# Batch 0's attention: normalising the output by spread row sums, alternating heads, and an earlier end of its rest

## The chip, the cores and the metric

The kernel runs on one core of a Trainium2 chip, as one launch. The metric is the device time of that launch in microseconds (us). The engines are PE (TensorE, the matrix engine, with PEld its weight loads), DVE (VectorE), ACT (ScalarE), POOL (GpSimd) and SP (which here issues DMA transfers). Each runs its own queue of instructions strictly in the order in which the program issued them, and waits at semaphores for the others.

## The reference, cut to what matters

```python
def _attn_ref(q, k, v, n_global, n_local):      # batch 2, heads 8, seq 768, head_dim 64
    scores = scale * np.matmul(q, k.transpose(0, 1, 3, 2))
    keep = is_global | is_local                  # 8 global keys, a band of 96 keys
    scores = np.where(keep, scores + bias, -1000000000.0)
    scores = scores - np.max(scores, axis=-1, keepdims=True)
    a = np.exp(scores)
    a = a / (np.sum(a, axis=-1, keepdims=True) + 1e-09)
    return np.matmul(a, v)

def _moe_ref(x, w_gate, w1, w2):                 # x 1536 x 512, 8 experts, d_ff 1024
    P = np.exp(x @ w_gate - max)                 # then 8 rounds of row and column sums
    for e in range(8):
        out += P[:, e:e + 1] * (np.maximum(x @ w1[e], 0.0) @ w2[e])

def _moe2_ref(x, w_in, w_out):                   # d_ff 2048
    h = x @ w_in
    return (h * (1.0 / (1.0 + np.exp(-1.702 * h)))) @ w_out
```

The attention's output, both batches under one another, is the x of the experts, and their sum is the x of the last network.

## The kernel before, in words

All products are of fp32 operands split into a high and a low part; each product is three matmuls (high by low, low by high, high by high). The first layer of every expert is done with seven products of block sums instead of eight products of blocks (operands of the tokens are B11, B21, B22, T1 to T4, those of the weights A11, A12, S1 to S4; each has an h and an l part).

**The attention** (`attention_banded`) goes through 48 works in order. A work is a batch b, a head pair hp (two heads, on partitions 0 to 63 and 64 to 127) and a tile i of 128 queries; a head pair has six works. For a step n of the loop the order of issue in the first phase is `ORDER[1] = "tsvrn"`:

- t, `turn` of work n - 3: the probabilities `a` are transposed on PE into a PSUM tile `pt` (L913) and, from i = 2 on, their columns for the global keys into `pg` (L921); ACT copies them to `ah` (L916) and `ag` (L925).
- s, `scores` of work n: for each head j three matmuls (L876) into a tile `s`, then DVE adds the bias and takes the row's extreme (L889), then ACT takes the exponential and sums the rows into `rs` (L892).
- v, `values` of work n - 4: PE multiplies by the values into `pv` (L954); after an odd i `put_x` copies two tiles' worth of it with ACT into the token matrix `xf` (L726, two copies of 64 partitions by 256).
- r, the rest of `turn`: DVE makes the low part `al` from `pt` and `ah` (L934).
- n, `norm` of work n - 1: DVE adds 1e-9 to the row sums (L899), takes the reciprocal (L900) and scales `a` with it, once for each head (L902).

Behind a work with i = 1 or i = 4, `prep_qk` transposes the next three tiles of keys and queries: PE into `pk` and `pq` (L812, L818), ACT into `kh` and `qh` (L813, L823), DVE into `kl` and `ql` (L814, L824), POOL copies the global keys (L827).

PSUM has eight banks, in four pools: `ps_s` 2, `ps_t` 2, `ps_v` 1, `ps_m` 3. `psum(kind)` says which pool a tile takes. In the first phase the scores go to m, and "p" (`pk`, `pq`) to s. `pt` and `pg` are both of kind "t". A tile can be written only when the readers of the tile that had its bank before are done.

**The phases.** In phase 1 PE does the attention of batch 0 and the first works of batch 1, up to the values of (0, 3, 3); meanwhile DVE, ACT and POOL already prepare the first weights (`first_weights`) and the first operands of the tokens of batch 0 (B11, T1). Then comes `mixture`: layer 1 of the first unit of an expert, with a list of side work that is issued between its products: the rest of batch 0's attention, then its last operands (`operands0`: B21, B22, T2, T3, T4), then batch 1's attention, and so on. `need(name)` issues all side work up to that name on the spot. In the scores of phase 1 one head's three matmuls stand before the other's; in phase 2 the heads alternate.

The first products of layer 1 are, in order, x (A11 by B11, tile `pl1x`), z (S1 by T1, `pl1z`), x again (A12 by B21) and y (S2 by T2, `pl1y`), all at L462.

Of the kernel before, what the change touches and what calls it, by code (L numbers as in the profile page):

```python
# [7 lines left out]
F32 = mybir.dt.float32  # L8
# [3 lines left out]
AF = mybir.ActivationFunctionType  # L12
ALU = mybir.AluOpType
# [3 lines left out]
P = 128  # L17
GK = 32
# [5 lines left out]
LT, LV = 3, 4  # L24
# [24 lines left out]
class Kernel:  # L49
# [495 lines left out]
    def psum(self, kind, shape, name):  # L545

        if kind == "2":
            self.turnover += 1
            kinds = {2: "m", 3: "sst", 4: "sstt"}[self.phase]
            kind = kinds[self.turnover % len(kinds)]  # L550
        elif self.phase == 1:
            kind = {"s": "m", "p": "s"}.get(kind, kind)
        kind = "t" if kind == "p" else kind
        p = {"s": self.ps_s, "t": self.ps_t, "v": self.ps_v, "m": self.ps_m}[kind]
        return p.tile(shape, F32, tag=kind, name=name)

# [69 lines left out]
    def mixture(self, side):  # L626


        side = list(side)
        done = set()  # L630
        debt = [0.0]

        def advance(steps=None):
            if not side:
                return
            debt[0] += side[0][2] if steps is None else steps
            while debt[0] >= 1 and side:
                debt[0] -= 1
                name, g, _ = side[0]
                try:  # L640
                    next(g)
                except StopIteration:
                    done.add(name)
                    side.pop(0)

        def need(name):
            while any(n == name for n, _, _ in side):
                advance(1.0)

        self.need = need  # L650
        self.ahead_done = False
        steps = self.steps
        NV = len(self.versions)
        nx = self.nx
        prev = None

        def second(step):
            v, u, b, lastv = step
            turn = (v, u) == self.ends[b]
            if turn and b == 0:  # L660
                self.xf2 = [self.xfp.tile([P, self.DC, self.S], F32, tag="xf", name="xf2_0")]
            for t, _ in enumerate(self.layer2(v, u, b)):
                advance()
                if turn and t >= LR:
                    self.retranspose(b, t - LR)
            if turn:
                side.insert(0, (f"again{b}", again(b), (1.2, 1)[b]))
            if lastv and v + 1 < NV:
                self.split_w2(v + 1)
                self.load_w2(v + 3)  # L670

        def again(b):

            self.operands_open(b, (self.xp0, self.xp1)[b], self.acc[b])
            for t in range(self.NT - LR, self.NT):
                self.retranspose(b, t)
                yield
            yield from self.operands(b, self.xf2[b], fine=True)

        for i, (v, u, b) in enumerate(steps):  # L680
            lastv = i + 1 == len(steps) or steps[i + 1][0] != v
            if u == 0 and b == 1:
                need("operands1")
            if (v, u) == self.ends[b] and b == 1:
                need("doubles")
                self.last()
            if (v, u) == self.starts[b]:
                need(f"again{b}")
            n = 0
            for k in self.layer1(v, u, b, first=i == 0):  # L690
                if i == 0 and n == 2:
                    need("operands0")
                if lastv and v + 1 < NV and n >= 1:
                    self.split_w1(v + 1, last)
                last = k
                n += 1
                advance()
            if lastv and v + 1 < NV:
                self.split_w1(v + 1, last)
                self.load_w1(v + 3)  # L700
                for _ in self.sum_weights(v + 2):
                    pass
            if prev is not None:
                combined = prev[1] == self.ue and prev[2] == 1
                if combined:
                    need("sinkhorn")
                second(prev)
                if prev[1] == 2 * self.ue - 1 and prev[2] == 0:
                    self.ahead_done = True
                if combined:  # L710
                    self.late()
                    side.append(("doubles", self.doubles(self.cv), 0.42))
            prev = (v, u, b, lastv)
        second(prev)


    def put_x(self, pv, b, hp, i):


        nc = self.nc  # L720
        if hp == 0 and i == 1:
            self.xf = self.xfp.tile([P, self.DC, self.S], F32, tag="xf", name=f"xf_{b}")
        ts_ = slice((i - 1) * P, (i + 1) * P)
        for j in range(2):
            r = slice(64 * j, 64 * j + 64)
            nc.scalar.activation(self.xf[r, hp, ts_].rearrange("p (s t) -> p s t", s=2), pv[r, :, j, :], AF.Copy)  # L726

    def slope(self, h):
        return 2.0 ** -(8.0 * (h + 1) / self.H)
# [1 line left out]
    def attention_open(self, ctx):  # L731
        nc, tc = self.nc, self.tc
# [3 lines left out]
        self.a_q = pool("a_q", 2)  # L736
        self.a_v = pool("a_v", 3)
        self.a_m = pool("a_m", 4)
        c = self.a_c

        self.bias = c.tile([P, 2 * W], F32, name="bias")
# [110 lines left out]
    def scores(self, b, hp, i):  # L852

        nc = self.nc
# [7 lines left out]
        else:  # L862
            keys, bias, wn = lambda x: x[:, (i - 1) * SLOT : (i - 1) * SLOT + W], self.bias[:, P : P + W], W
        a = self.a_a.tile([P, 2, W], F32, tag="a", name=f"a_{b}_{hp}_{i}")
        rs = self.a_m.tile([P, 2], F32, tag="rs", name=f"rs_{b}_{hp}_{i}")

        rows = [slice(64 * j, 64 * j + 64) for j in range(2)]
        passes = [(ql, self.kh), (qh, self.kl), (qh, self.kh)]
# [6 lines left out]
            x, y = passes[n]  # L875
            nc.tensor.matmul(o, x[rows[j], i % 3, :], keys(y[rows[j]]), start=(n == 0), stop=(n == 2))  # L876

        if self.phase > 1:
            for n in range(3):
                for j in range(2):  # L880
                    product(j, n)
        for j in range(2):
            if self.phase == 1:
                for n in range(3):
                    product(j, n)
            s = a[:, j, :wn]
            o, x = (pairs(s, P), pairs(ps[j], P)) if i == 1 else (s, ps[j])
            m = self.a_m.tile([P, 1], F32, tag="m", name=f"m_{b}_{hp}_{i}_{j}")
# [2 lines left out]
            )  # L891
            nc.scalar.activation(s, s, AF.Exp, bias=m, scale=-1.0, accum_out=rs[:, j : j + 1])  # L892
            yield
        self.aa[b, hp, i] = a, rs, wn

    def norm(self, b, hp, i):
        nc = self.nc
        a, rs, wn = self.aa[b, hp, i]
        nc.vector.tensor_scalar(rs, rs, 1e-9, None, op0=ALU.add)  # L899
        nc.vector.reciprocal(rs, rs)  # L900
        for j in range(2):
            nc.vector.tensor_scalar(a[:, j, :wn], a[:, j, :wn], rs[:, j : j + 1], None, op0=ALU.mult)  # L902

    def turn(self, b, hp, i):

# [10 lines left out]
        nc.scalar.activation(ah[:, :n], pt, AF.Copy)  # L916
        ag = None
        if i >= 2:
            pg = self.psum("t", [GK, 2, P], f"pg_{b}_{hp}_{i}")
            for j in range(2):  # L920
                nc.tensor.transpose(pg[:, j, :], a[:, j, P:SLOT], self.ident)  # L921

# [17 lines left out]
    def values(self, b, hp, i):  # L940
# [12 lines left out]
        for n, (x, y) in enumerate(mm):  # L953
            nc.tensor.matmul(o, x, y, start=(n == 0), stop=(n == len(mm) - 1))  # L954
        if i % 2 == 1:
            self.put_x(self.pv, b, hp, i)

    def attention_banded(self):

        nc = self.nc  # L960
        self.aq, self.av, self.vg = {}, {}, {}
        self.aa, self.at = {}, {}
        pairs = [(b, hp) for b in range(self.B) for hp in range(self.HP)]
        work = [(b, hp, i) for b, hp in pairs for i in range(self.NT)]
        tables = self.tables()
# [6 lines left out]
        for n in range(len(work) + LV):  # L972
# [3 lines left out]
            for o in ORDER[self.phase]:  # L976
# [5 lines left out]
                    rest = self.turn(*work[n - LT])  # L982
                if o == "n" and 1 <= n <= len(work):
                    self.norm(*work[n - 1])
                if o == "r" and rest is not None:
                    rest()
                    yield
# [257 lines left out]
```

## Time and profile before

| what | before |
|---|---|
| time, median of 3 runs (lowest to highest) | 1463.09 us (1460.62 to 1464.42) |
| run that was profiled | 1463.75 us, of which 1461.8 us is the span from the first to the last instruction |
| granted TensorE clock, mean over the span | 0.987 |
| busy, share of the span | PE 96%, DVE 69%, POOL 60%, ACT 44% |
| chain that ended last | PE 70% of the span |

The time lies 1.95 us above the span in the profiled execution. The first phase lasts until about 95 us, a fifteenth of the span; the rest is nearly all the experts' products. The granted clock is 1.00 at 2.4 GHz and about half at 1.2 GHz.

### The profile page before, as it was taken

How to read it: one execution, taken by the hardware profiler on the slowest of the kernel's cores; microseconds unless marked ns; L12 is line 12 of the kernel's file. 1: busy time of each engine (PE TensorE's matmuls, PEld its weight loads, DVE VectorE, ACT ScalarE, POOL GpSimd, SP SyncE). 2: the span in 40 equal slices, each digit the busy share in tenths (PEclk: the TensorE clock that was granted, in tenths of full speed). 3: DMA queues.
4: the chain of work that ended last, by engine and by line, in shares of the span. 5: the costliest groups of instructions: out<-in, count | busy, mean ns of one | idle time of the engine just before them, and what ended most of it. 6: DMA issues, size and time to landing. Idle time of an engine off the chain costs nothing.

```text
span 1461.8 us, 20827 instructions
## 1 busy us (share of the span) xinstructions
PE 1409.9 (96%) x7295; PEld 1244.0 (85%) x7295; DVE 1005.5 (69%) x1847; ACT 642.1 (44%) x1511; POOL 870.7 (60%) x1003
## 2 busy tenths in 40 slices
PE   7899999998999999999999999999999979999998
PEld 5667888787899998998998998998989868899897
DVE  7987887577567777677777777767754466556655
ACT  5676766343443333333333343343334456444332
POOL 4745555657685556655566555666556596666642
PEclk9989999999999999999999999999999999999999
DMA  6322210111122222212222212222101110111002
GB/s 158 79 49 62 74 47 30 58 59 58 58 88 86 73 87 73 81 57 73 72 87 66 86 63 68 77 83 87 44 29 44 44 44 29 44 41 32 30 0 87
DMA packets 94225, 91.62 MB, mean 63 GB/s; under 512 B 41888, under 2 KB 71584, under 8 KB 94112
## 3 DMA queue, kind: packets, MB, share of 16 engines
q1 hardware_dynamic: 94112, 90.21, 19.7%
q8 instruction: 59, 0.97, 0.3%
q14 instruction: 54, 0.44, 0.1%
HBM read 78.66 MB, written 11.53 MB: 62 GB/s over the span
## 4 chain that ended last, share of the span: by engine, by line
PE 70%; DVE 2%; ACT 1%; POOL 1%; issue 1%; DVEq 0%; ACTq 0%
PE pl L515 37%; PE pl1x L462 9%; PE pl1y L462 9%; PE pl1z L462 9%; PE pl1w L462 5%; DVE sg L431 1%; ACT sg L428 0%; DVE acc L526 0%; DVE acc L298 0%; PE pr L542 0%; ACT hh L210 0%; DVE p L416 0%; POOL s L203 0%; DVE u L416 0%; POOL hl L216 0%
## 5 line engine op out<-in xcount | busy, mean ns | idle before, releaser
L515 PE MATMUL pl<-w2h,hl 128*128 128x512 f32 x960 | 303.6, 398 | 14.2 <-DVE accx L524 5.4
L526 DVE SCALAR_TENSOR_TENSOR acc<-pl,pr,acc 128x512 f32<-128x512 f32 x312 | 233.2, 749 | 120.8 <-PE pl L515 118.9
L515 PE MATMUL pl<-w2l,hh 128*128 128x512 f32 x960 | 299.5, 393 | 1.0 <-POOL w2l L216 1.0
L515 PE MATMUL pl<-w2h,hh 128*128 128x512 f32 x960 | 298.8, 393 | 0.0
L216 POOL TENSOR_TENSOR w2l<-r,w2h 128x512 fp32r<-128x512 f32 x100 | 133.6, 1357 | 191.2 <-ACT w2h L210 177.0
L515 PEld LDWEIGHTS pl<-w2h,hl 128*128 128x128 f32 x960 | 177.0, 189 | 49.1 <-DVE accx L524 6.6
L515 PEld LDWEIGHTS pl<-w2l,hh 128*128 128x128 f32 x960 | 181.7, 189 | 41.4 <-POOL w2l L216 1.9
L515 PEld LDWEIGHTS pl<-w2h,hh 128*128 128x128 f32 x960 | 181.5, 189 | 39.0
L210 ACT ACTIVATE w2h<-r 128x512 fp32r<-128x512 f32 x98 | 56.5, 624 | 201.6 <-PE pl L515 163.2
L438 POOL TENSOR_TENSOR hl<-u,hh 128x384 fp32r<-128x384 f32 x100 | 108.6, 1094 | 36.9 <-ACT hh L435 36.6
L469 ACT ACTIVATE p<-pl1x 128x384 f32<-128x384 f32 x80 | 39.2, 490 | 160.4 <-PE pl1x L462 147.6
L438 POOL TENSOR_TENSOR hl<-p,hh 128x384 fp32r<-128x384 f32 x50 | 50.8, 1015 | 97.0 <-ACT hh L435 97.0
L416 DVE TENSOR_TENSOR u<-p,pl1y 128x384 f32<-128x384 f32 x86 | 47.5, 552 | 79.0 <-PE pl1y L462 67.6
L216 POOL TENSOR_TENSOR hl<-sg,hh 128x384 fp32r<-128x384 f32 x64 | 67.1, 1049 | 54.9 <-ACT hh L210 54.1
L434 ACT ACTIVATE p<-p 128x384 f32<-128x384 f32 x50 | 26.3, 526 | 134.9 <-DVE p L416 134.9
L216 POOL TENSOR_TENSOR S3l<-s,S3h 128x256 fp32r<-128x256 f32 x50 | 38.5, 770 | 75.6 <-ACT S3h L210 62.9
L443 DVE SCALAR_TENSOR_TENSOR hl<-pl1x,hh 128x384 fp32r<-128x384 f32 x64 | 35.6, 557 | 66.7 <-ACT hh L440 66.3
L203 POOL TENSOR_TENSOR s<-r 128x256 f32<-128x256 f32 x100 | 78.8, 788 | 0.0
L434 ACT ACTIVATE u<-u 128x384 f32<-128x384 f32 x100 | 51.9, 519 | 50.7 <-DVE u L416 50.5
L892 ACT ACTIVATE a<-a,m 128x288 f32<-128x288 f32 (+2 forms) x96 | 48.1, 501 | 42.5 <-DVE m L889 42.5
L532 DVE TENSOR_TENSOR acc<-pl,acc 128x512 f32<-128x512 f32 x84 | 54.2, 682 | 13.8 <-PE pl L515 12.7
L216 POOL TENSOR_TENSOR A22l<-r,A22h 128x256 fp32r<-128x256 f32 x50 | 45.0, 900 | 24.0 <-ACT A22h L210 24.0
(266 smaller groups left out, 3415.9 us busy)
## 6 DMA issues: line engine op xcount, KB each, us to landing
r<-in_moe_w_dram SPq DMA_DIRECT2D x82, 512.0 KB, 3.5
r<-d SPq DMA_DIRECT2D x18, 512.0 KB, 3.7
d<-in_moe_w_in_dram SPq DMA_DIRECT2D x16, 512.0 KB, 4.5
d<-cx SPq DMA_DIRECT2D x32, 256.0 KB, 2.2
d<-in_moe_w_out_dram SPq DMA_DIRECT2D x16, 512.0 KB, 4.3
out_dram<-acc SPq DMA_DIRECT2D x12, 256.0 KB, 2.0
k<-in_k_dram SPq DMA_DIRECT2D x28, 96.0 KB, 2.3
q<-in_q_dram SPq DMA_DIRECT2D x28, 96.0 KB, 2.4
```

The costliest lines, as they stand in the source:

```text
L203: nc.gpsimd.tensor_tensor(out=o, in0=x, in1=y, op=op)
L210: nc.scalar.activation(hi, x, AF.Copy)
L216: e.tensor_tensor(out=lo, in0=x, in1=f(hi), op=ALU.subtract)
L416: add = lambda o, x, y: nc.vector.tensor_tensor(out=o, in0=x, in1=y, op=ALU.add)
L434: nc.scalar.activation(c, c, AF.Relu)
L438: nc.gpsimd.tensor_tensor(out=l, in0=c, in1=f(h), op=ALU.subtract)
L462: nc.tensor.matmul(ps, x[:, d, :], y[:, d, :], start=(new and i == 0 and d == 0), stop=(i == 2 and d == 1), skip_group_check=True)
L469: nc.scalar.activation(p1, ps, AF.Copy)
L515: nc.tensor.matmul(ps, x[:, c, ts_], y, start=(i == 0 and c == 0), stop=(i == 2 and c == 1))
L526: nc.vector.scalar_tensor_tensor(out=acc, in0=ps, scalar=self.pr[:, tt, e : e + 1], in1=acc, op0=ALU.mult, op1=ALU.add)
L532: nc.vector.tensor_tensor(out=acc, in0=ps, in1=acc, op=ALU.add)
L892: nc.scalar.activation(s, s, AF.Exp, bias=m, scale=-1.0, accum_out=rs[:, j : j + 1])
```

## The change

It has four parts.

1. `psum`: in phase 1 "p" (`pk`, `pq`) takes banks of m, which the scores also take, and the new kind "g" (`pg`, and the new `pb`) takes those of s. `pt` has the two t banks for itself.
2. `scores`: the heads' products alternate in phase 1 too.
3. For batch 0 the probabilities are no longer scaled. The row sums of two works (i even and odd) lie in one tile `rs` of 128x4; behind the odd one `norm` adds 1e-9 and takes the reciprocal once, and POOL spreads the four columns to `rw`, 128x256 (each 64 times). `spread`, right behind the `turn` of the odd work, transposes `rw` on PE into `pb` (two transposes, L923) and ACT copies it to `rb` (L925 of the changed kernel). `put_x` then multiplies `pv` by `rb` on DVE (L730, two of 64x256) instead of copying it on ACT. Batch 1 stays as it was.
4. In the first layer 1 the rest of batch 0's attention and `operands0` are issued behind the first product instead of the third.

```diff
-            kind = {"s": "m", "p": "s"}.get(kind, kind)
-        kind = "t" if kind == "p" else kind
+            kind = {"s": "m", "p": "m", "g": "s"}.get(kind, kind)
+        kind = "t" if kind in "pg" else kind
...
-                if i == 0 and n == 2:
+                if i == 0 and n == 0:
                     need("operands0")
...
-            nc.scalar.activation(self.xf[r, hp, ts_].rearrange("p (s t) -> p s t", s=2), pv[r, :, j, :], AF.Copy)
+            o = self.xf[r, hp, ts_].rearrange("p (s t) -> p s t", s=2)
+            if rb is None:
+                nc.scalar.activation(o, pv[r, :, j, :], AF.Copy)
+            else:
+                nc.vector.tensor_tensor(out=o, in0=pv[r, :, j, :], in1=rb[r], op=ALU.mult)
...
-        if self.phase > 1:
-            for n in range(3):
-                for j in range(2):
-                    product(j, n)
+        for n in range(3):
+            for j in range(2):
+                product(j, n)
         for j in range(2):
-            if self.phase == 1:
-                for n in range(3):
-                    product(j, n)
...
-        nc.vector.tensor_scalar(rs, rs, 1e-9, None, op0=ALU.add)
-        nc.vector.reciprocal(rs, rs)
+        if b == 0 and i % 2 == 0:
+            return
+        o = rs.rearrange("p s j -> p (s j)") if b == 0 else rs[:, i % 2]
+        nc.vector.tensor_scalar(o, o, 1e-9, None, op0=ALU.add)
+        if b == 0:
+            w = self.a_b.tile([P, 4, self.D], F32, tag="rw", bufs=1, name=f"rw_{b}_{hp}_{i}")
+            nc.vector.reciprocal(o, o)
+            nc.gpsimd.tensor_scalar(w, o[:, :, None].to_broadcast([P, 4, self.D]), 1.0, 1.0, op0=ALU.mult, op1=ALU.mult)
+            self.rb[b, hp, i] = w
+            return
+        nc.vector.reciprocal(o, o)
         for j in range(2):
-            nc.vector.tensor_scalar(a[:, j, :wn], a[:, j, :wn], rs[:, j : j + 1], None, op0=ALU.mult)
+            nc.vector.tensor_scalar(a[:, j, :wn], a[:, j, :wn], o[:, j : j + 1], None, op0=ALU.mult)
+
+    def spread(self, b, hp, i):
+        nc = self.nc
+        w = self.rb[b, hp, i].rearrange("p s d -> p (s d)")
+        pb = self.psum("g", [P, 2, P], f"pb_{b}_{hp}_{i}")
+        for s in range(2):
+            nc.tensor.transpose(pb[:, s, :], w[:, s * P : s * P + P], self.ident)
+        rb = self.a_b.tile([P, 2, P], F32, tag="rb", name=f"rb_{b}_{hp}_{i}")
+        nc.scalar.activation(rb, pb, AF.Copy)
+        self.rb[b, hp, i] = rb
...
-            pg = self.psum("t", [GK, 2, P], f"pg_{b}_{hp}_{i}")
+            pg = self.psum("g", [GK, 2, P], f"pg_{b}_{hp}_{i}")
...
+                if o == "t" and LT <= n and n < len(work) and work[n - LT][0] == 0 and work[n - LT][2] % 2 == 1:
+                    self.spread(*work[n - LT])
```

Three places show how instructions move. In their rows the batch is left out of a name: `s_1_2_0_19899` is the score tile of head pair 1, tile 2, head 0, and the last number is that of the buffer.

PE in phase 1, head pair 1, behind the preparation of its second half of keys and queries, before the change:

```order
L812 MATMUL pk_19861<-ident,k_19604 128x128 x3
L818 MATMUL pq_19867<-ident,q_19607 128x128 x3
L913 MATMUL pt_0_5_19884<-ident,a_0_5_19732 128x128 x4
L921 MATMUL pg_0_5_19892<-ident,a_0_5_19732 32x128 x2
L876 MATMUL s_1_2_0_19899<-kh,ql_19708 128x288
L876 MATMUL s_1_2_0_19899<-kl,qh_19707 128x288
L876 MATMUL s_1_2_0_19899<-kh,qh_19707 128x288
L876 MATMUL s_1_2_1_19906<-kh,ql_19708 128x288
L876 MATMUL s_1_2_1_19906<-kl,qh_19707 128x288
L876 MATMUL s_1_2_1_19906<-kh,qh_19707 128x288
```

The same place in the changed kernel:

```order
L817 MATMUL pk_19854<-ident,k_19602 128x128 x3
L823 MATMUL pq_19860<-ident,q_19605 128x128 x3
L937 MATMUL pt_0_5_19877<-ident,a_0_5_19730 128x128 x4
L945 MATMUL pg_0_5_19885<-ident,a_0_5_19730 32x128 x2
L923 MATMUL pb_0_5_19890<-ident,rw_0_5_19808 128x128 x2
L883 MATMUL s_1_2_0_19897<-kh,ql_19706 128x288
L883 MATMUL s_1_2_1_19899<-kh,ql_19706 128x288
L883 MATMUL s_1_2_0_19897<-kl,qh_19705 128x288
L883 MATMUL s_1_2_1_19899<-kl,qh_19705 128x288
```

The two transposes of `pb` have come in ahead of the scores, and the second head's first product stands right behind the first head's. `pk`, `pq` and the two score tiles follow one another through the three banks of m, so the second score tile takes the bank that `pk` had.

DVE in phase 1, around the end of head pair 1, before:

```order
L889 ISA a_2_1_20144,m_2_1_1_20157<-s_2_1_1_20153,bias 128x256
L889 ISA m_2_1_1_20157 128x1
L934 TENSOR_TENSOR al_1_4_20137<-pt_1_4_20131,ah_1_4_20136 128x512
L899 TENSOR_SCALAR rs_2_0_20099<-rs_2_0_20099 128x2
L900 RECIPROCAL rs_2_0_20099<-rs_2_0_20099 128x2
L902 TENSOR_SCALAR a_2_0_20098<-a_2_0_20098,rs_2_0_20099 128x128 x2
L814 TENSOR_TENSOR kl<-pk_20178,kh 128x3x128
L824 SCALAR_TENSOR_TENSOR ql_20189<-pq_20184,qs,qh_20188 128x384
```

And in the changed kernel:

```order
L892 ISA a_2_1_20142,m_2_1_1_20154<-s_2_1_1_20145,bias 128x256
L892 ISA m_2_1_1_20154 128x1
L730 TENSOR_TENSOR xf_19751<-pv_1_2_20116,rb_1_3_20094 64x256 x2
L958 TENSOR_TENSOR al_1_4_20135<-pt_1_4_20129,ah_1_4_20134 128x512
L819 TENSOR_TENSOR kl<-pk_20171,kh 128x3x128
L829 SCALAR_TENSOR_TENSOR ql_20182<-pq_20177,qs,qh_20181 128x384
```

The scaling between `al` and `kl` is gone, and the two multiplications of `put_x` have come in ahead of `al`.

PE at the start of the mixture, before (the products x and z, then the scores and transposes of the attention, then x again):

```order
L462 MATMUL pl1x_0_20844<-B11h_20288,A11h_20000 128x384 x2
L812 MATMUL pk_20857<-ident,k_20543 128x128 x3
L818 MATMUL pq_20863<-ident,q_20546 128x128 x3
L462 MATMUL pl1z_0_20879<-T1h_20296,S1l_20201 128x384 x2
L462 MATMUL pl1z_0_20879<-T1l_20297,S1h_20200 128x384 x2
L462 MATMUL pl1z_0_20879<-T1h_20296,S1h_20200 128x384 x2
L876 MATMUL s_0_2_0_20892<-kh,ql_20684 128x288
```

And in the changed kernel, first behind x, and then where z now stands:

```order
L462 MATMUL pl1x_0_20841<-B11h_20285,A11h_19998 128x384 x2
L817 MATMUL pk_20854<-ident,k_20536 128x128 x3
L823 MATMUL pq_20860<-ident,q_20539 128x128 x3
L883 MATMUL s_0_2_0_20878<-kh,ql_20682 128x288
```

```order
L978 MATMUL pv_3_4_20915<-ag_3_5_20903,vg_20422 128x256
L883 MATMUL s_0_4_0_20978<-kh,ql_20865 128x288
L883 MATMUL s_0_4_1_20980<-kh,ql_20865 128x288
L883 MATMUL s_0_4_0_20978<-kl,qh_20864 128x288
L883 MATMUL s_0_4_1_20980<-kl,qh_20864 128x288
L883 MATMUL s_0_4_0_20978<-kh,qh_20864 128x288
L883 MATMUL s_0_4_1_20980<-kh,qh_20864 128x288
L462 MATMUL pl1z_0_20989<-T1h_20293,S1l_20194 128x384 x2
```

The products z and x (A12 by B21) have moved from ahead of the last values of batch 0 (`pv_3_4`) to behind them and behind the scores (0, 4) of batch 1, just ahead of y.

## Rows read from the trace of the kernel before

**Rows 1.** The page: its span, and the chain that ended last by engine.
```profile
span 1461.8 us, 20827 instructions
...
PE 70%; DVE 2%; ACT 1%; POOL 1%; issue 1%; DVEq 0%; ACTq 0%
```

**Rows 2.** Windows: stretch, length, busy PE, PEld, DVE, ACT, POOL, then granted clock.
```profile
54.00:66.00 12.00, 6.85 (x49) 4.71 (x48) 11.86 (x29) 6.29 (x20) 9.10 (x12) 1.00 0.33 84
66.00:77.00 11.00, 11.00 (x48) 8.02 (x48) 8.53 (x24) 6.22 (x19) 6.97 (x12) 0.54 0.26 77
...
88.00:95.20 7.20, 6.82 (x37) 4.86 (x37) 6.91 (x20) 5.89 (x19) 5.97 (x9) 0.76 0.09 21
...
104.00:120.00 16.00, 13.28 (x67) 11.00 (x66) 13.09 (x31) 8.86 (x24) 4.86 (x7) 0.79 0.11 26
```

**Rows 3.** Waits of PE, 14 to 95.2 us: total, times, longest.
```profile
PE pg L921 <- DVE al L934: 4.2, 5, 1.9
PE pv L954 <- ACT xf L726: 1.2, 1, 1.2
PE pg L921 <- DVE rs L899: 1.2, 1, 1.2
PE pt L913 <- DVE a L902: 1.0, 2, 0.8
```

**Rows 4.** Groups by line, 14 to 104 us, DVE and ACT.
```profile
L902 DVE TENSOR_SCALAR a<-a,rs 128x288 f32<-128x288 f32 (+2 forms) x53 | 27.5, 560 | 0.9
...
L726 ACT ACTIVATE xf<-pv 64x256 f32<-64x256 f32 x22 | 8.2, 372 | 1.4 <-PE pv L954 1.2
```

**Rows 5.** Timeline of DVE and POOL at 54 us; line L934 alone (minimum/median/maximum ns).
```profile
53.65 2.58 DVE L902 TENSOR_SCALAR a<-a,rs 128x256 f32<-128x256 f32 x2
...
54.27 1.81 POOL L216 TENSOR_TENSOR B11l<-xf,B11h 128x768 fp32r<-128x768 f32 x1
...
L934 DVE TENSOR_TENSOR al<-pt,ah x24: 414/682/693, 18.7 to 101.0; 128x512 fp32r<-128x512 f32 x20, 128x256 fp32r<-128x256 f32 x4
```

**Rows 6.** Timeline around a preparation of keys and queries.
```profile
48.96 0.55 PE L812 MATMUL pk<-ident,k 128*128 128x128 f32 x3
...
49.41 0.41 POOL L214 TENSOR_SCALAR A22h<-r 128x256 fp32r<-128x256 f32 x1
...
49.67 0.60 PE L913 MATMUL pt<-ident,a 128*128 128x128 f32 x4
...
50.11 0.38 PE L921 MATMUL pg<-ident,a 128*32 128x128 f32 x2
...
50.42 0.41 PE L876 MATMUL s<-kh,ql 64*128 64x288 f32 x2
...
50.63 0.55 DVE L814 TENSOR_TENSOR kl<-pk,kh 128x384 fp32r<-128x384 f32 x1
...
51.03 0.39 PE L954 MATMUL pv<-al,vh 128*128 128x256 f32 x1
```

**Rows 7.** Timeline around the next preparation.
```profile
58.96 0.49 PE L812 MATMUL pk<-ident,k 128*128 128x128 f32 x3
...
61.69 0.41 PE L876 MATMUL s<-kh,ql 64*128 64x288 f32 x2
...
63.46 0.54 DVE L814 TENSOR_TENSOR kl<-pk,kh 128x384 fp32r<-128x384 f32 x1
```

**Rows 8.** Timeline of PE at the start of the mixture.
```profile
96.92 0.60 PE L462 MATMUL pl1z<-T1h,S1l 128*128 128x384 f32 x2
...
98.15 0.41 PE L876 MATMUL s<-kh,ql 64*128 64x288 f32 x2
...
98.74 0.66 PE L913 MATMUL pt<-ident,a 128*128 128x128 f32 x4
...
106.43 0.44 PE L462 MATMUL pl1y<-T2h,S2l 128*128 128x384 f32 x1 [1.16 <-ACT T2h L210]
...
107.63 0.45 PE L462 MATMUL pl1y<-T2l,S2h 128*128 128x384 f32 x1 [0.58 <-DVE T2l L216]
```

More of the change, by code (lines that the diff above doesn't have):

```diff
@@ L714, in mixture, with put_x @@
         second(prev)
-    def put_x(self, pv, b, hp, i):
+    def put_x(self, pv, b, hp, i, rb=None):
         nc = self.nc
@@ L738, in attention_open @@
         self.a_m = pool("a_m", 4)
+        self.a_b = pool("a_b", 2)
         c = self.a_c
@@ L864, in scores @@
         a = self.a_a.tile([P, 2, W], F32, tag="a", name=f"a_{b}_{hp}_{i}")
-        rs = self.a_m.tile([P, 2], F32, tag="rs", name=f"rs_{b}_{hp}_{i}")
+        if i % 2 == 0:
+            self.rs = self.a_m.tile([P, 2, 2], F32, tag="rs", name=f"rs_{b}_{hp}_{i}")
+        rs = self.rs[:, i % 2]
         rows = [slice(64 * j, 64 * j + 64) for j in range(2)]
@@ L893, in scores @@
             yield
-        self.aa[b, hp, i] = a, rs, wn
+        self.aa[b, hp, i] = a, self.rs, wn
     def norm(self, b, hp, i):
@@ L955, in values @@
         if i % 2 == 1:
-            self.put_x(self.pv, b, hp, i)
+            self.put_x(self.pv, b, hp, i, self.rb.pop((b, hp, i), None))
     def attention_banded(self):
@@ L961, in attention_banded @@
         self.aq, self.av, self.vg = {}, {}, {}
-        self.aa, self.at = {}, {}
+        self.aa, self.at, self.rb = {}, {}, {}
         pairs = [(b, hp) for b in range(self.B) for hp in range(self.HP)]
```

## The prediction

> **What bounds the kernel now.** I read the page first: the span is 1461.8 us, and the chain that ended last is PE for 70% and nobody else for more than 2% [rows 1]. So an edit is worth what it does to PE's own queue: PE's work, PE's idle time, and the clock that PE was granted. The change touches the first phase and the start of the mixture, up to about 120 us, so I read the windows of that part next. Between 54 and 66 us PE worked 6.85 of 12 us, while DVE was busy 11.86: there DVE is the bound. Behind it, from 66 to 77 us, PE never stood, but the granted clock was 0.54, that is the lower level (1.2 GHz) nearly throughout; from 88 to 95.2 us it was 0.76 [rows 2]. Then PE's waits: from 14 to 95.2 us it stood 4.2 us at `pg` for DVE's `al`, 1.2 at `pv` for ACT's copies of `put_x`, 1.2 at `pg` behind DVE's row sums, 1.0 at `pt` for the scaled probabilities [rows 3]; 7.6 us in all. The largest of them is a matter of banks as much as of DVE: `pg` takes the t bank of an earlier `pt`, which is free only when DVE has made its `al`. What is late on DVE is the scaling: 53 instructions of L902, 27.5 us, more than any other line of that engine between 14 and 104 us [rows 4].
>
> **What there is to win in the first phase.** Parts 1 and 3 of the change take both causes away: `pg` no longer shares with `pt`, and 48 of the scalings (the others are batch 1's) go, 48 x 0.56 = 27 us of DVE. In their place DVE gets 24 multiplications of 64x256; the nearest row is the smallest `al`, 128x256 also out of PSUM, 0.414 us [rows 5], so 24 x 0.41 = 10 us. DVE is left with 17 us less. ACT loses the 24 copies of 0.372 [rows 4], 9 us, and gets 12 copies of 128x256; no path. POOL gets 12 spreads, which I price by its copy of 128x256, 0.41 us [rows 6], 5 us in all.
>
> The bound of the gain is then: 7.6 us of waits; plus the clock, 11.00 x (1 - 0.54) = 5.1 us and 7.20 x (1 - 0.76) = 1.7 us [rows 2], since the low clock in the first of these follows the stretch in which PE stood most; less PE's new work. That is 24 transposes of `pb`. Four transposes lie between 49.67 and 50.11 us [rows 6], 0.11 each, so 2.6 us. 7.6 + 6.8 - 2.6 = 11.8, **about 12 us**.
>
> **What the change puts in.** First the banks. `pk`, `pq` and the scores now follow one another through three banks, so the second head's first product behind a preparation takes the bank of `pk`, which DVE leaves when `kl` is made. Before, nothing in the scores waited for that. The wait is in PE's queue, and as the heads now alternate, all of the two heads' other products, then the values, stand behind it, and behind these ACT's exponentials. What it costs: in the one case `pk` starts at 48.96, the scores come at 50.42 and `kl` ends at 50.63 + 0.55 = 51.18: 0.7 us late. In the other `pk` starts at 58.96 and `kl` ends at 63.46 + 0.54 = 64.00, 5.0 us later, where PE's own way from `pk` to the scores is 1.46 us, a wait of 3.5 us [rows 6, 7]. But both had scalings ahead of `kl` in DVE's queue, and two copies of `put_x` ahead of `kh` in ACT's; these are gone, and two multiplications of 0.41 can stand there instead. The lower bound is 0, the upper 3.5; I take 0.5, nearer to the first case, and there are eight such places (two for each of four head pairs): **4 us lost**.
>
> Second, `put_x` on DVE waits for PE's `pv` and for `rb`; behind it in DVE's queue stands `al`, which the next values need. There is a step (some 3 us) between `al` and the values that use it, so most of the 0.82 us is covered. I take 0.2 us for each of 11 pairs of works, between 0 (all covered) and 0.82: **2 us lost**.
>
> Third, `pb` waits on PE for POOL's `rw`, which stands in POOL's queue behind pieces of up to 1.81 us [rows 5]. `norm` of the odd work is issued two steps before its `spread`, so POOL has some 6 us for it. I take nothing, up to 1.8 us for each of 11; this is the slow rival below.
>
> Alternating heads alone I put at nothing. Phase 2 alternated already: its group began at 98.15 and the next instruction at 98.74, 0.59 us; the group of phase 1, one head behind the other, took from 50.42 to 51.03, 0.61 us [rows 6, 8].
>
> **The start of the mixture.** Before, PE stood 1.16 us and then 0.58 us at y, for T2h and T2l [rows 8], because the last values of batch 0, their `put_x` and the sums of blocks came just ahead of it; and the window from 104 to 120 us has a clock of 0.79 [rows 2], 16 x 0.21 = 3.4 us. Now z and the second x stand between those values and y: z took from 96.92 to 98.15 in the trace, 1.23 us [rows 8], so the two are some 2.4 us of cover, more than the 1.74 of the waits. But z also covered something where it was: from `pk` to the scores (0, 2) the copies into `kh`, `kl` and `ql` are made, and z lay just between. Without it PE stands there for about 1.0 us. 1.74 - 1.0 = 0.7 without the clock, 4.1 with all of it. I take a third of the clock's part: **2 us won**.
>
> **The sum.** 12 - 4 - 2 + 2 = 8 us. The profiled execution took 1463.75 us, 1.95 more than its span, so it becomes 1455.8. It lies 0.66 us above the median of the runs shown (1463.09), so against the median the same sum gives 1455.1; I say **1455.5 us**. A change within 0.3%, 4.4 us, can't be told from none: faster means below 1458.7, slower above 1467.5.
>
> **A rule for what remains on DVE.** `al`, which reads PSUM and one tile of SBUF, never took over 0.693 us, also beside POOL's long pieces, while two scalings took 2.58 us beside one of 1.81 [rows 5]. The multiplications of `put_x` read as `al` does, so I expect them at 0.4 us everywhere; stretched as those scalings were, at 1.3 each, the six or so beside POOL's longest pieces would cost up to 5 us. The Trainium skill states this as a rule, in "SBUF — State Buffer", section "Who interferes with whom": DVE and GpSimd share one pair of ports as an exclusive lock, and a DVE instruction with at most one input in SBUF, outside the two-port modes, is not held. The trace agrees as far as `al` goes; by the rule the sum stays.
>
> **Rivals.** *All of it comes back.* If neither `kl` nor `put_x` is late (DVE has 17 us less to do) and the clock stays up: 12 to 12 + 4 = 16 us won, 1447 to 1451. For it: DVE was the only bound from 54 to 66 us. Against it: the clock was 0.76 from 88 us on, where PE stood less than half a us in 7 [rows 2]. Chance 0.18.
>
> *The banks take it back.* If `kl` is late by 1.0 to 1.5 us at each of the eight places, 8 to 12 us are lost there, and the gain is 12 - 8 - 2 + 2 = 4 us down to 0: 1459 to 1463. For it: the 3.5 us of the second case [rows 7], where POOL's pieces and the scalings met. Against it: the scalings are gone. Chance 0.15.
>
> *Slower: `pb` waits for POOL.* PE's queue holds `pb` ahead of the scores; if `rw` stands behind two pieces of 1.8 us and the wait is 1.8 us at each of 11 spreads, 20 us are lost against the 8 won: 1467.5 to 1475. It decides from 8/11 = 0.7 us each for no gain, and from 12.4/11 = 1.1 us each for slower. For it: POOL was busy 9.10 of 12 us from 54 to 66 [rows 2]. Against it: two steps of lead, and elsewhere POOL had room. Chance 0.08.
>
> *Alternating does more.* If the second head's products lay wholly beside the first's, three of 0.14 us would vanish in each of 24 works, 10 us more: about 1445. A page, "TensorE: Matmul & The Clock Gate", section "🎯 Why this matters for your kernels" of the Trainium skill, says that matmuls of few rows on different row groups run concurrently; that speaks for it. The 0.59 against 0.61 us says that it is so in both orders or in neither. Chance 0.02.
>
> **How the numbers follow.** My forecast (4.4 to 12 us won, 1451 to 1458.7) has 0.57. Faster: 0.57 + 0.18 + 0.02 = 0.77. Within 0.3%: the banks' 0.15, and 0.01 of the last of the slow rival: 0.16. Slower: 0.07, the rest of it. The range goes from the whole gain, a us rounded down, to the banks' case and leaves out the slow rival and the last: 1446 to 1462.
>
> **What would show it.** In the changed profile: PE's busy time from 54 to 66 us up from 6.85 and the clock behind it at 1.00; no wait at `pg` for `al`; waits at the second head's first product for `kl`, some 0.5 us, at eight places; none at `pb` for POOL; `put_x` at 0.4 us; the first layer-1 product at about 85 us instead of 95.17; a wait of about 1 us at the scores (0, 2), and none at y for T2. The prediction is wrong if the clock falls elsewhere for as long as before, if `pb` waits, or if `kl` is late by 1.5 us and not by a half.

## The result, and the profile after

The changed kernel takes 1475.46 us (median of 9 runs, 1470.19 to 1477.15), the kernel before 1463.09 (9 runs, 1460.62 to 1467.65): a ratio of 1.0077, 95% interval 1.0064 to 1.009, some 11 us **slower** (12.4 between the two medians). The forecast was 8 us faster. The profiled execution took 1476.41 us, 1474.6 of it the span, 12.8 more than before [rows 1].

Where it went is read first from one line of DVE that has the same 312 instructions in both kernels, the sums over experts (L526), from its first and last start; before the change, and after it:

```profile
L526 DVE SCALAR_TENSOR_TENSOR acc<-pl,pr,acc x312: 734/751/754, 396.8 to 1207.8; 128x512 f32<-128x512 f32 x156
```

```profile
L526 DVE SCALAR_TENSOR_TENSOR acc<-pl,pr,acc x312: 736/751/753, 408.4 to 1220.6; 128x512 f32<-128x512 f32 x156
```

408.4 - 396.8 = 11.6 us are lost before the first of them, and 1.2 more by the last. So nearly all of the loss is made ahead of 400 us: where the change works, up to about 120 us, and, as the experiments show, behind that too, although from 120 to 400 us none of its four parts adds an instruction.

PE's waits in the changed kernel from 14 to 95.2 us, against [rows 3]:

```profile
PE s L883 <- DVE kl L819: 3.7, 7, 1.4
PE pb L923 <- POOL rw L910: 2.6, 1, 2.6
PE pv L978 <- DVE al L958: 1.7, 5, 0.4
PE pv L978 <- PE s L883: 0.2, 1, 0.2
```

Every wait of [rows 3] is gone, and others of 8.2 us stand in their place. The windows, against [rows 2]:

```profile
54.00:66.00 12.00, 9.72 (x69) 7.19 (x68) 9.89 (x31) 8.21 (x25) 9.82 (x13) 1.00 0.43 108
66.00:77.00 11.00, 9.11 (x43) 6.69 (x44) 3.88 (x15) 3.75 (x13) 9.49 (x16) 0.68 0.22 69
77.00:88.00 11.00, 10.71 (x67) 7.90 (x65) 6.88 (x24) 7.65 (x23) 3.18 (x5) 0.85 0.27 61
...
104.00:120.00 16.00, 14.83 (x67) 11.76 (x68) 11.19 (x31) 7.33 (x20) 4.07 (x6) 0.68 0.09 22
```

From 54 to 66 us PE did work more, 9.72 us for 6.85, as foretold. But the stand and the low clock only came later: from 66 to 77 us PE was idle for 1.9 us at a clock of 0.68, and DVE had so little to do (3.88 of 11 us) that it can't be the bound. The timeline of PE, DVE and POOL shows what happened:

```profile
59.72 2.59 POOL L216 TENSOR_TENSOR B11l<-xf,B11h 128x768 fp32r<-128x768 f32 x1
...
62.37 0.18 DVE L909 RECIPROCAL rs<-rs 128x4 f32<-128x4 f32 x1
...
63.06 0.40 PE L883 MATMUL s<-kh,ql 64*128 64x288 f32 x1 [1.38 <-DVE kl L819]
...
65.66 1.80 POOL L216 TENSOR_TENSOR T1l<-acc,T1h 128x768 fp32r<-128x768 f32 x1
67.43 0.40 POOL L910 TENSOR_SCALAR rw<-rs 128x256 f32<-128x256 f32 x1
...
67.89 0.44 PE L923 MATMUL pb<-ident,rw 128*128 128x128 f32 x2 [2.60 <-POOL rw L910]
```

The row sums for `rw` were ready at 62.37 + 0.18 = 62.55 us. PE came to `pb` at 67.89 - 2.60 = 65.29, 2.7 us later. POOL came to `rw` only at 67.43, behind B11l, two small pieces of the gate's weights, two weight pieces and the two of T1, and PE stood 2.6 us at `pb`. That is the slow rival's mechanism, at one place and not at eleven. Then the start of the mixture, PE alone:

```profile
98.79 0.41 PE L883 MATMUL s<-kh,ql 64*128 64x288 f32 x2
...
100.20 0.66 PE L937 MATMUL pt<-ident,a 128*128 128x128 f32 x4 [0.74 <-DVE kl L819]
...
103.11 0.41 PE L923 MATMUL pb<-ident,rw 128*128 128x128 f32 x2 [1.99 <-ACT ag L949]
...
110.39 1.01 PE L462 MATMUL pl1z<-T1h,S1l 128*128 128x384 f32 x2
...
115.24 0.51 PE L462 MATMUL pl1y<-T2h,S2l 128*128 128x384 f32 x2
```

There is no wait for T2 any more, as foretold, but 0.74 + 1.99 us ahead of it, and behind them, from 104 to 120 us, a clock of 0.68, where it was 0.79 [rows 2]. The 1.99 us were not in my sum: in the mixture `pk`, `pq`, `pt`, `pg` and `pb` all share the two t banks, `pb` takes the one that `pg` has, and `pg` is free only when ACT has copied it, which ACT does behind the exponentials of the scores (0, 2), for which DVE must first make `kl` and `ql`. PE waits at `pb` for a whole round through DVE and ACT.

### The profile page after: what moved, and what is told of

It is laid out like the page before. It is cut to its first block, busy times and chain, and to the rows that moved or that the text cites. A ratio compares the mean times of both kernels' runs of the same rounds, so it can differ in the third digit from the quotient of the medians.

```text
span 1474.6 us, 20850 instructions
## 1 busy us (share of the span) xinstructions
PE 1418.5 (96%) x7319; PEld 1251.4 (85%) x7319; DVE 988.2 (67%) x1799; ACT 637.0 (43%) x1499; POOL 875.9 (59%) x1015
## 4 chain that ended last, share of the span: by engine, by line
PE 84%; DVE 7%; ACT 3%; POOL 3%; issue 2%; POOLq 0%; DVEq 0%; ACTq 0%
PE pl L515 41%; PE pl1y L462 10%; PE pl1x L462 10%; PE pl1z L462 10%; PE pl1w L462 5%; PE pv L978 3%; PE s L883 1%; PE pt L937 1%; DVE hl L443 1%; DVE u L416 1%; DVE al L958 1%; ACT a L895 1%; DVE sg L431 0%; ACT hh L440 0%; DVE acc L298 0%
## 5 line engine op out<-in xcount | busy, mean ns | idle before, releaser
L526 DVE SCALAR_TENSOR_TENSOR acc<-pl,pr,acc 128x512 f32<-128x512 f32 x312 | 233.2, 749 | 121.6 <-PE pl L515 119.9
L416 DVE TENSOR_TENSOR u<-u,pl1w 128x384 f32<-128x384 f32 x74 | 40.8, 552 | 23.4 <-PE pl1w L462 23.0
```

What stands on the lines that cost most here:

```text
L416: add = lambda o, x, y: nc.vector.tensor_tensor(out=o, in0=x, in1=y, op=ALU.add)
L526: nc.vector.scalar_tensor_tensor(out=acc, in0=ps, scalar=self.pr[:, tt, e : e + 1], in1=acc, op0=ALU.mult, op1=ALU.add)
```

## The experiments

Ratios are to the kernel before, in the same comparison, with the 95% interval. The median of the kernel before differs by up to 1.2 us from one comparison to the next, so differences between comparisons are rounded.

**The parts alone.** Part 4 on the kernel before, and the changed kernel without it:

```diff
-                if i == 0 and n == 2:
+                if i == 0 and n == 0:
                     need("operands0")
```

> The kernel before with only part 4 (rest of batch 0 issued behind the first product of layer 1). Theory A, the order at the start of the mixture is the main loss: between the transposes of keys and queries and the scores (0, 2) PE has nothing else, 1 us idle, z and the second x cover T2 (1.7 us), but the clock falls earlier; and all of batch 1's attention comes at other places of the products. Slower by 4 to 8 us, 1467 to 1471. Theory B, the loss is in phase 1 (banks, waits for the spread sums) and in the new transposes: no change, 1461 to 1465.

> The changed kernel with part 4 undone. Theory A: 1475.5 less 5 to 9 us, 1466 to 1470, and PE no longer waits 2 us at the spread's transposes in the mixture. Theory B: within 3 us of the changed kernel, 1473 to 1478.

Part 4 alone: 1468.92 us, 1.0047 (1.0033 to 1.0061), 7 us slower. The other three parts, without it: 1468.21, 1.0043 (1.0022 to 1.0064), 6 us slower. The loss has two halves, and within the intervals they add up. Then part 1 and part 2 alone, with the lines of the change's diff:

> The kernel before with only part 1 (keys, queries and scores share three banks; the global keys' transposes take the s banks). Theory A: the wait of pg for al (4.2 us) goes, the second head's product waits for kl at eight places; since DVE still scales, kl is late by 1 us and more there: 1461 to 1467, no clear change. Theory B: slower by 5 us or more, 1468 and above.

> The kernel before with only part 2 (heads alternate in phase 1). Both theories: no change, 1460 to 1466; a gain of some 10 us (1453) would show that a second head's products run beside the first's only in this order.

The banks: 1464.81, 1.0016 (1.0002 to 1.0031), 2 us slower. Alternating: 1462.57, 1.0000 (0.9988 to 1.0012), nothing. So what is left of the second half, some 4 us, comes with part 3, which was to win 12.

**Part 4: not the moved products.** Next I put the rest one product later (the number 1 instead of 0), and then kept part 4 and held batch 1's attention back for as many products as part 4 brings it forward:

> The kernel before with the rest of batch 0 issued behind the second product z (part 4 puts it behind the first, 1468.9). Theory A, what part 4 loses is the cover that z gave between pk and the scores: 1461 to 1464, as before or a little better. Theory B, it loses by the place of batch 1's attention among the products, or by the second x that no longer stands ahead of the values: 1466 to 1470.

```diff
                 n += 1
-                advance()
+                if i > 0 or n > 2:
+                    advance()
```

> The kernel before with part 4, and batch 1's attention held back for two products, so that behind the start of the mixture everything stands in the order of before. Theory A, part 4 loses by the shifted place of batch 1's attention among the products: 1462 to 1465. Theory B, it loses at the start alone (no cover between pk and the scores, and the clock): 1467 to 1470, as with part 4 alone (1468.9).

Behind z: 1469.59, 1.0043 (1.0026 to 1.006), no better, so giving z's cover back does not help. Held back: 1463.47, **1.0002** (0.999 to 1.0014), no loss at all. In that kernel z and x stand exactly where part 4 puts them, and PE has the long wait at the mixture's start too:

```profile
PE pt L914 <- DVE kl L815: 1.9, 1, 1.9
```

Only what comes later is in the order of before. The longest waits of PE between 118 and 400 us show it, in order: before, the changed kernel, part 4 alone, part 4 with the attention held:

```profile
PE pl L515 <- DVE accx L524: 5.4, 3, 3.7
PE pc L387 <- DVE cs L383: 2.2, 5, 0.9
PE pl1z L462 <- DVE p L416: 2.0, 1, 2.0
PE pk L812 <- DVE al L934: 1.1, 1, 1.1
```

```profile
PE pc L387 <- DVE cs L383: 4.4, 3, 1.6
PE pl L515 <- DVE accx L524: 3.9, 1, 3.9
PE pk L817 <- DVE al L958: 3.3, 2, 2.2
PE pl1z L462 <- DVE p L416: 2.5, 1, 2.5
PE pg L945 <- DVE ql L829: 1.0, 1, 1.0
```

```profile
PE pc L387 <- DVE cs L383: 4.4, 3, 1.6
PE pl L515 <- DVE accx L524: 3.9, 1, 3.9
PE pk L812 <- DVE al L934: 3.3, 2, 2.2
PE pl1z L462 <- DVE p L416: 2.5, 1, 2.5
PE pg L921 <- DVE ql L824: 1.0, 1, 1.0
```

```profile
PE pl L515 <- DVE accx L524: 5.5, 3, 3.7
PE pc L387 <- DVE cs L383: 2.0, 4, 0.9
PE pl1z L462 <- DVE p L416: 1.9, 1, 1.9
PE pk L813 <- DVE al L935: 1.2, 2, 1.1
```

The second and the third are the same to a tenth, the first and the fourth nearly so. All waits of these 282 us together are 14.3, 19.0, 18.8 and 14.9 us, so 3.9 of the 5 to 7 us between the last two are waits here. `advance` moves the side work by a fixed number of steps with each product; when the rest of batch 0 is done two products earlier, batch 1's attention is two products further on at every later product, up to 250 us and through the gate's sums behind it, and meets other transposes and weights there.

**What DVE's relief is worth.** I left the scaling out, on the kernel before and on the changed kernel without part 4 and without a spread (the new banks and the alternating heads), so that batch 0 stays unnormalised and nothing is put in the scaling's place. No kernel from here on has part 4:

```diff
         a, rs, wn = self.aa[b, hp, i]
+        if b == 0:
+            return
```

> The kernel before without the division for batch 0 (L899 to L902 left out, nothing in their place: batch 0's attention stays unnormalised). Theory A, DVE's work was the bound of phase 1: 7.6 us of waits and up to 6.8 us of clock come back, 1449 to 1456. Theory B, the chain from the scores through DVE and ACT back to PE and the banks are the bound, and the clock falls behind each longer wait: 1460 to 1470.

> The changed kernel without part 4 (1468.2), without the division for batch 0 and without the spread (no rw, pb, rb; put_x copies on ACT). What the spread costs by itself is the difference to 1468.2: Theory A (the spread's waits and its 24 transposes hold the loss in phase 1): 1456 to 1461. Theory B (the waits for kl hold it): 1465 to 1468.

With the banks of before: 1454.71, 0.9945 (0.9927 to 0.9964), 8 us faster. With the new banks: 1457.11, 0.9964 (0.995 to 0.9978), 5 us faster. The two windows of [rows 2] that held the loss before, in the first of these kernels:

```profile
54.00:66.00 12.00, 10.59 (x79) 7.75 (x78) 7.34 (x23) 9.60 (x31) 11.50 (x16) 1.00 0.25 69
66.00:77.00 11.00, 10.86 (x80) 8.10 (x79) 6.06 (x19) 9.85 (x30) 5.98 (x11) 1.00 0.59 145
```

So the view on DVE was right: without the scaling PE works on and the clock stays at 1.00. And the price of the spread, with all that belongs to it, can be read off: 1468.21 - 1457.11 = **11 us** (1.0043 against 0.9964), more than the relief gives.

**What of the spread costs.** Three edits of the changed kernel without part 4: one kernel makes `rw`, `pb` and `rb` and doesn't use them (batch 0 stays unnormalised); one makes `rw` on DVE; one issues the spread a step later (with two buffers for `rw` and one for `rb`):

```diff
-            self.put_x(self.pv, b, hp, i, self.rb.pop((b, hp, i), None))
+            self.rb.pop((b, hp, i), None)
+            self.put_x(self.pv, b, hp, i)
```

> The changed kernel without part 4, with the spread made as there (rw, pb, rb) and not used: put_x copies on ACT as before the change (batch 0 stays unnormalised). Theory A, the cost is what stands in PE's queue (24 transposes, 2.6 us; the wait for POOL, 2.6 us, and the clock behind it; the wait for ag in the mixture): 1464 to 1468. Theory B, the cost is put_x on DVE, which waits for the values and for rb with al behind it: 1458 to 1462.

```diff
-            nc.gpsimd.tensor_scalar(w, o[:, :, None].to_broadcast([P, 4, self.D]), 1.0, 1.0, op0=ALU.mult, op1=ALU.mult)
+            nc.vector.tensor_scalar(w, o[:, :, None].to_broadcast([P, 4, self.D]), 1.0, 1.0, op0=ALU.mult, op1=ALU.mult)
```

> The changed kernel without part 4, with rw made by DVE instead of POOL (12 instructions of some 0.4 us). Theory A: the 2.6 us wait for POOL goes, and with it the low clock behind it, the 1.8 us in the mixture stay: 1462 to 1465. Theory B: 1467 to 1470.

```diff
                 if o == "v" and n >= LV:
+                    if work[n - LV][0] == 0 and work[n - LV][2] % 2 == 1:
+                        self.spread(*work[n - LV])
                     self.values(*work[n - LV])
```

> The changed kernel without part 4, with spread issued one step later, just ahead of the values that need it (two buffers for rw, one for rb). Theory A: PE waits neither for POOL's rw nor for ag, and the clock does not fall behind it: 1468.2 - 2.6 - 1.8 - 3 = 1460 to 1463. Theory B: still 1466 to 1469.

Unused: 1467.61, 1.0031 (1.0017 to 1.0044), still 10 us above the kernel without a spread. So `put_x` on DVE is not the main cost; what is left are POOL's `rw`, PE's `pb` and ACT's `rb`. The waits that came with them are in PE's queue. PE's waits of that kernel from 14 to 124 us have the same two at `pb`:

```profile
PE pb L923 <- POOL rw L910: 2.6, 1, 2.6
PE pb L923 <- ACT ag L949: 1.8, 1, 1.8
```

On DVE: 1465.95, 1.002 (1.001 to 1.003), 2 to 3 us less than with POOL, not clear of the intervals, the wait for `rw` gone (and one of 2.45 us for `kl` in its place). A step later: 1470.89, 1.0058 (1.0041 to 1.0075), no gain: `pb` no longer waits, but now `put_x` waits for `rb` (9.2 us at eight places), `al` behind it is late, and PE stands 5.9 us at `pv`. That miss showed me that the wait only changes its place.

**The banks.** The banks of before with the spread (`pb` beside the scores, in the banks of m), and the same with the late spread:

```diff
-            kind = {"s": "m", "p": "m", "g": "s"}.get(kind, kind)
+            kind = {"s": "m", "p": "s", "g": "m"}.get(kind, kind)
...
-            pg = self.psum("g", [GK, 2, P], f"pg_{b}_{hp}_{i}")
+            pg = self.psum("t", [GK, 2, P], f"pg_{b}_{hp}_{i}")
```

> The changed kernel without part 4 (1468.2) and with the banks of before: pk and pq in the s banks, pg in the t banks, only pb beside the scores. Theory A, the waits of PE at the spread's transposes (2.6 us for POOL, then a low clock; 1.8 us in the mixture) hold the loss: they stay, so within 2 us of 1468, although the scores no longer wait for kl (4.3 us in the trace of that kernel), because pg waits for al again. Theory B, the banks hold it: 4 us less, 1464.

> The edits of the two kernels above with the banks of before and the late spread together. Theory A: PE's new waits are all gone, and what DVE is relieved of is seen: 1455 to 1460, faster than the kernel before. Theory B: the old waits of pg for al and new ones take their place: 1462 to 1466.

1479.95, 1.0113 (1.0085 to 1.0141), and 1479.72, 1.0123 (1.0104 to 1.0142): 17 us slower than before, and outside both theories. In the first, PE stands 7.2 us at `pg` for `al`, which with the spread comes behind `put_x` on DVE. The first long one, and the windows from there:

```profile
25.07 0.39 PE L945 MATMUL pg<-ident,a 128*32 128x128 f32 x2 [1.60 <-DVE al L958]
```

```profile
25.00:42.00 17.00, 16.93 (x88) 12.36 (x88) 7.69 (x29) 8.39 (x26) 5.45 (x10) 0.70 0.50 110
42.00:54.00 12.00, 10.23 (x71) 7.50 (x69) 7.20 (x25) 7.59 (x23) 8.67 (x20) 0.85 0.30 67
54.00:66.00 12.00, 12.00 (x64) 9.05 (x64) 6.84 (x23) 6.45 (x19) 4.53 (x9) 0.72 0.15 35
```

Part 1 is thus what makes part 3 bearable.

**The wait for `kl`.** Three kernels tried to take it away: the preparation issued ahead of the values (in the kernel with `rw` on DVE), the same with the last two works of batch 0 scaled as before, and, as a control, the new banks with it but with the scaling kept:

```diff
             for o in ORDER[self.phase]:
+                if o == "v" and early and i == 1:
+                    yield from self.prep_qk(2 * pair + 1)
+                if o == "v" and early and i == 4 and pair + 1 < len(pairs):
+                    yield from self.prep_qk(2 * pair + 2)
```

> The changed kernel without part 4, with rw on DVE (1466.0), and in phase 1 the preparation of keys and queries issued ahead of the values of its step instead of at the step's end, so that PE has the values to do while kl is made and DVE makes kl and ql ahead of put_x and al. Theory A, the banks' wait for kl (5.3 us in the trace of that kernel, one of 2.5) and the clock behind its longest hold what is left of the loss: 1466 - 5 to 8 = 1458 to 1461, faster than before. Theory B, the wait only moves to al, which is now behind kl and ql: 1464 to 1468.

> The same, with the last two works of batch 0 (tiles 4 and 5 of head pair 3, whose turns and values fall into the mixture) scaled and copied as before, without a spread. Theory A: PE no longer waits 1.7 us at the spread for ag in the mixture, and the clock there is as before: 2 to 4 us below the kernel before this one, 1455 to 1458. Theory B: the wait at y for T2 grows by as much: no difference.

> The kernel before with the new banks (1464.8) and the early preparation, but with the scaling of before on DVE. If the waits for banks and not DVE's work are what bounds phase 1: as fast as the kernel with the spread and the early preparation, 1458 to 1461. If DVE's scaling bounds it: 1462 to 1466.

All three got slower: 1476.85, 1.0096 (1.008 to 1.0112); 1475.29, 1.0082 (1.0067 to 1.0097); 1475.99, 1.0092 (1.0074 to 1.0109). PE's waits from 14 to 124 us in the first:

```profile
PE pv L978 <- DVE al L958: 8.8, 10, 1.4
PE s L883 <- DVE kl L819: 2.5, 5, 1.1
```

DVE waits in its queue for ACT's `kh` (11.4 us at nine places), with `al` behind it. The control is not explained by this: its waits of PE from 14 to 124 us come to 12 us, as with the new banks alone, and what differs is the clock, 0.87 against 0.98 over 14 to 95 us. Why it fell there no run shows. Last, `pk` alone in an s bank and the last two works as before, again with `rw` on DVE:

```diff
-            kind = {"s": "m", "p": "m", "g": "s"}.get(kind, kind)
+            kind = {"s": "m", "p": "m", "k": "s", "g": "s"}.get(kind, kind)
```

> The changed kernel without part 4, rw on DVE (1466.0), pk alone in an s bank, which leaves the scores no wait for kl behind the preparations at i = 4 and, at i = 1, moves it to pb or away, and the last two works of batch 0 scaled as before. Theory A: half of the 5.3 us for kl and the 1.7 us at the spread in the mixture go: 1461 to 1463.5. Theory B: the waits only move to pb and pg: 1464 to 1468.

1464.49, 1.0015 (1.0002 to 1.0028), against 1.002 (1.001 to 1.003) without this edit: the waits for `kl` are down from 5.3 us to 0.8, at `pg`, and those at `pv` are up from 1.7 to 4.7, those at `pb` from 1.7 to 2.2. No version with a spread beat the kernel before.

**A relief that adds nothing.** Before the division a row's largest entry is exp(0) = 1, its sum is at least 1, and adding 1e-9 to it changes no fp32 number, so L899 can go:

```diff
-        nc.vector.tensor_scalar(rs, rs, 1e-9, None, op0=ALU.add)
         nc.vector.reciprocal(rs, rs)
```

> The kernel before without L899: a row's largest probability is 1, so its sum is at least 1 and adding 1e-9 leaves an fp32 number as it is. It takes 9 us from DVE in phase 1 and nothing is added. If DVE's work bounds phase 1 (the whole scaling, some 40 us, was worth 8): 1 to 3 us faster, 1459 to 1461. If only chains bound it: no change.

1459.77 us, 0.9987 (0.9973 to 1.0001): some 2 us faster, with an interval that just reaches no change. It is the best whole kernel that I have, and not clear of the measurement.

## Why the prediction was wrong, step by step

- **"The bound of the gain is about 12 us": right in kind, much too large, the first step that failed.** Before the 2.6 us of new transposes are taken off, this term is 7.6 of waits + 6.8 of clock = 14.4 us. The kernels without the scaling won 8 (with the banks of before, where 3.0 us of `pg`'s waits for `al` stay) and 5 (with the new banks, where 14.4 - 4 = 10.4 were foretold). The clock's part was read from one trace as if it were fixed. But four kernels issue the same instructions up to the first product (the one before, part 4 alone, the rest behind z, part 4 with the attention held), and their clock from 66 to 77 us is 0.54 [rows 2], 0.84, 0.55 and 1.00. The trace that the forecast was made from is one of the two in which it fell far.
- **"First the banks ... 4 us lost": right.** 3.7 us at seven places up to 95 us, 0.5 us each; part 1 alone cost 2, and in its trace the 4.2 us at `pg` for `al` are gone.
- **"`put_x` on DVE ... 2 us lost": right, if anything too much.** 0.422 us each (24 of them, 416 to 429 ns), also beside POOL's pieces of 1.0 us; none fell beside the longest. PE waited 1.7 us at `pv` for `al`. Without `put_x` on DVE the ratio is 1.0031 instead of 1.0043, at most 2 us and within the intervals.
- **"`pb` waits on PE for POOL's `rw` ... I take nothing": the second step that failed.** I counted two steps and 6 us of lead and held them against single pieces of 1.81 us. By the order of issue `norm` of work w is the last thing in step w + 1 and its `spread` stands near the front of step w + 3, so one step lies between, and at the place of the wait the trace has 2.7 us. POOL had seven pieces in a row there, from 59.72 to 67.43 us, and B11l took 2.59. And I looked at `pb` in phase 1 alone: its bank in the mixture, the 1.99 us behind ACT's `ag`, is in none of my terms. I had priced the spread at 2.6 of transposes + 2 for `put_x` = 4.6 us; it cost 11. Waits of 2.6 + 1.99 us, the transposes, and the low clock behind the waits are what the traces have for it; how the 11 us divide among them is not shown. The rival had the mechanism of the first wait, but priced it as eleven equal ones. That its time, 1467.5 to 1475, lies next to the measured one is luck: part 4's loss is not in it.
- **"The start of the mixture ... 2 us won": the third step that failed, and the largest.** It measured 7 us lost by itself, 5 in the changed kernel (1.0077 against 1.0043). My terms at the place itself were fair: the waits for T2 went, one ahead of `pt` came (0.74 us, or 1.9 in part 4 alone), and with batch 1's attention held these cancel (1.0002). What I left out is that `need` doesn't only move the rest: it lets all side work behind it start two products earlier. Of a paced list, I priced the item that moved and not its followers.
- **"Alternating heads alone I put at nothing": right**, 1.0000. The rival, that the second head's products would run beside the first's only in this order, does not hold here. Whether they run side by side in both orders, as the page "TensorE: Matmul & The Clock Gate" of the Trainium skill, section "🎯 Why this matters for your kernels", states of matmuls with few rows on distinct row groups, this comparison cannot show.

In sum: 8 won by the relief, 2 to 3 lost by the banks with it (0.9964 against 0.9945), 11 by the spread, 5 to 7 by part 4, together 10 to 13 slower; measured 11. Against the forecast the relief fell short by some 6 us, the spread cost 6 more, and the start of the mixture 7 to 9 more.

What stays open: the last 1.2 us, between the first and the last of L526. That stretch took 811.0 us before and 812.2 in the changed kernel, but 813.2 with the new banks alone and 813.3 with the attention held, so it can't be put down to the change. Why batch 1's attention meets worse waits at just this shift I can name (the rows above) but could not have foretold; I tried only one other shift, and it was as bad.

## What to carry to other kernels

A new instruction in the queue of the engine that bounds can cost more than its duration: price what it waits for at every place where it is issued, with the banks and the queues of that stage, and sum the whole run of work ahead of it on its producer. Count its lead step by step in the order of issue. When an item of a paced side list is moved, everything behind it in the list moves too; hold the followers in place first, and then judge the move. And try the relief alone, without its replacement, before writing the replacement: it bounds what may be paid for it.

## What the runs showed of the hardware that I had not expected

In some traces PE's clock fell to the lower level behind a single wait and stayed there for many microseconds, while as much or more waiting in several pieces left it up in another. In the kernel with the old banks one wait of 1.60 us at 25.07 us stands ahead of a stretch of 17 us with a mean granted clock of 0.70 in which PE never stood; in the kernel with the early preparation PE was idle for 2.85 of the same 17 us, in four waits of 0.39 to 1.37 us, at a clock of 1.00:

```profile
25.00:42.00 17.00, 14.15 (x98) 10.33 (x98) 12.47 (x42) 9.56 (x31) 6.08 (x10) 1.00 0.53 109
```

In the first of them the low clock cost an estimated 17 x 0.3 = 5.1 us, more than the wait itself. But the wait alone does not decide it. With the attention held PE waits for 1.90 us at 66.16 us, as the kernel before does at 65.94, and the clock from 66 to 77 us is 1.00 and not 0.54 [rows 2]:

```profile
66.16 0.40 PE L922 MATMUL pg<-ident,a 128*32 128x128 f32 x2 [1.90 <-DVE al L935]
```

```profile
66.00:77.00 11.00, 10.50 (x73) 7.39 (x74) 10.72 (x33) 8.35 (x27) 7.21 (x12) 1.00 0.47 122
```

So the clock of a stretch, read from one trace, is one draw of several. With it and the waits around it, the four kernels that issue the same instructions up to the first product came to that product at these times (in the order before, part 4 alone, the rest behind z, the attention held):

```profile
95.17 0.62 PE L462 MATMUL pl1x<-B11h,A11l 128*128 128x384 f32 x2
```

```profile
90.71 0.62 PE L462 MATMUL pl1x<-B11h,A11l 128*128 128x384 f32 x2
```

```profile
95.86 0.62 PE L462 MATMUL pl1x<-B11h,A11l 128*128 128x384 f32 x2
```

```profile
90.59 0.62 PE L462 MATMUL pl1x<-B11h,A11l 128*128 128x384 f32 x2
```

What the two waits at `pb` cost beyond their 4.6 us is for that reason not shown singly.

POOL's own pieces stretch too: B11l took 1.81 us before [rows 5] and 2.59 in the changed kernel. No run shows why.
